# The second unit's v issued from ScalarE's queue instead of the sync engine, in attention followed by two MLPs

## The chip, the cores and the metric

One core of a Trainium2 chip. The metric is the device time of one execution of the whole kernel in microseconds (us), as the median of several runs.

## The reference

Inputs are q, k and v of 8 batches, 8 heads, 576 positions and 64 features, in 32-bit floats, and the weights of two MLPs (512 to 2048 to 512). What is computed, cut to what matters:

```python
q_s = softmax(q, axis=-1)            # over the 64 features, sum + 1e-9
k_s = softmax(k, axis=2)             # over the 576 positions, sum + 1e-9
kv  = einsum('bhsd,bhse->bhde', k_s, v)
x   = einsum('bhsd,bhde->bhse', q_s, kv)   # laid out as 4608 x 512
h = x @ w_in;  g = h * clip(h + 3, 0, 6) / 6;  x = g @ w_out     # first MLP
h = x @ w2_in; g = h * sigmoid(h);             out = g @ w2_out  # second MLP, 4608 x 512
```

## The kernel before, in words

The matmuls of the MLPs run at the rate of a one-pass format. To keep 32-bit accuracy each operand is split into an upper part and the rest, and each product is made of three matmuls. The 4608 tokens are nine blocks of 512. The stages are: `first_block` (the attention for block 0, the conversion of the first MLP's weights and the first MLP of block 0, with attention units of block 1 in between), `middle` (the rest of the first MLP and the attention, in an order written out in the table `MIDDLE`), and `second_mlp` (fixed passes, most of the time). Only the order of the first stage is planned, at build time.

**A unit** u of attention is a pair of heads of one token block. Units 0 to 3 give block 0. Its steps, each one method with its line: loads of k (L355, L359), v (two DMAs at L366 and a tail at L370) and q (L381); on VectorE the maxima (`q_max` L488, `k_max` L419 to L421); on TensorE `k_turn` L426 and, behind VectorE's `k_peak` L432, `k_spread` L438; the subtractions (`q_sub` L496 on GpSimd, `k_sub` L447 on VectorE); the exponentials on ScalarE (`q_exp` L506, `k_exp` L457); the sums and the normalisation of q (`q_norm` L522 on GpSimd); `q_turn` L530 and `q_copy` L555; the product k·v (`kv_mm` L466 on TensorE, `kv_sum` L474 and L475 on VectorE, `kv_scale` L483 on ScalarE); `x_mm` L567 on TensorE, its upper part copied by ScalarE (`x_upper` L581) and the rest made either on VectorE (L586) or by one more matmul and a copy (`x_rest` L594, `x_lower_copy` L601 on ScalarE). Matmuls at L933 on a tile `busy` are filler without a result, early in the stage.

**A weight** comes by a DMA on the sync engine (SP; L161 for w_in into `wi_early`, L155 for w_out into `wo_early`) and is split by `Conv`: two ScalarE steps (L176, L180), three VectorE steps (L188, L195, L199), ScalarE's `upper` (L216), then the rest (L220) on VectorE or GpSimd.

**One f** of the first MLP (f = 0 to 15, 128 of the 2048 hidden features): `mm1`, 12 matmuls at L613 into one of **two** PSUM banks `h`; the gate, which is `relu` L626 (ScalarE, into the **only** buffer `r`), `times_h` L653 (VectorE, reads `r`), `upper` L644 (ScalarE), `rest` L659 (one matmul), `lower_copy` L664 (ScalarE, gives the bank back); then `mm2`, 12 matmuls at L688.

**What sets the order.** `unit`, the weight conversions and the f steps add jobs to a `Plan`: an engine, an estimated duration in us, a key (how early it is wanted), the jobs it depends on, and the buffer tags that it takes and gives back. `plan.run` then works through them like a clock with one job at a time on every engine. Whatever each engine can start gets started in the order of the keys. The jobs are emitted in the planned order, and on the chip each engine runs its instructions in that order and waits at the first that isn't ready. A load counts as a job of 1.9 us of the queue it is put on (`"SP"` or `"AQ"`, ScalarE's queue). The instructions themselves, their number and their operands, do not depend on the plan.

Of the kernel before, what the change touches and what calls it, by code (L numbers as in the profile page):

```python
# [82 lines left out]
def efficient_attention_then_two_mlps(  # L83
# [267 lines left out]
    def load_k(u, eng=nc.sync):  # L351
        b, pr = divmod(u, NP)
        t = kbuf[u] = kbuf.get(u, kbuf[u % 2])
        src = k[b, 2 * pr : 2 * pr + 2]
        eng.dma_start(  # L355
            t[:, :, 0:KCH, :],
            src[:, 0 : KCH * P].rearrange("h (p j) d -> p h j d", j=KCH),
        )
        eng.dma_start(t[0:TAIL, :, KCH, :], src[:, KCH * P :].rearrange("h p d -> p h d"))  # L359

    def load_v(u, eng=nc.sync):
        b, pr = divmod(u, NP)
        t = vbuf[u] = vbuf.get(u, vbuf[u % 2])
        src = v[b, 2 * pr : 2 * pr + 2]
        for h in range(2):
            eng.dma_start(  # L366
                t[:, 0:KCH, h, 0:D],
                src[h, 0 : KCH * P].rearrange("(p j) d -> p j d", j=KCH),
            )
        eng.dma_start(  # L370
            t[0:TAIL, KCH, :, 0:D],
            src[:, KCH * P :].rearrange("h p d -> p h d"),
        )

    def load_q(u, eng=nc.sync):
        j, pr = divmod(u, NP)
        t = early.pop(("q", u), None)
        if t is None:
            t = att.tile([P, 2, NCH, D], F32, tag="q", bufs=2, name="qraw")
        for p0, n, b, s0 in parts(j):  # L380
            eng.dma_start(  # L381
                t[p0 : p0 + n],
                q[b, 2 * pr : 2 * pr + 2, s0 : s0 + NCH * n, :].rearrange(
                    "h (p i) d -> p h i d", i=NCH
                ),
            )
        qt[u] = t
# [97 lines left out]
    def q_max(u):  # L485
        t = qt[u]
        m = tiny.tile([P, 2, NCH, 1], F32, tag="qm", bufs=2, name="qm")
        nc.vector.tensor_reduce(out=m[:, :, :, 0], in_=t, op=ALU.max, axis=AX.X)  # L488
        live["qm", u] = m
# [14 lines left out]
    def q_exp(u):  # L504
        e = live["qe", u]
        nc.scalar.activation(e, e, AF.Exp)  # L506

    def q_sum(u):
        e = live["qe", u].rearrange("p i h d -> p (i h) d")
        s = tiny.tile([P, 2 * NCH, 1], F32, tag="qs", bufs=2, name="qs")  # L510
        nc.vector.tensor_reduce(out=s[:, :, 0], in_=e, op=ALU.add, axis=AX.X)
        live["qs", u] = s
# [280 lines left out]
    class Plan:  # L793
# [7 lines left out]
        def add(self, eng, us, key, fn, deps=(), take=(), give=(), port=False):  # L801
            self.jobs.append(
                (eng, us, key, fn, [d for d in deps if d is not None], list(take), list(give), port)
            )
            return len(self.jobs) - 1
# [104 lines left out]
    def first_block():  # L910
# [5 lines left out]
        def load(u, key, what, eng="SP", deps=()):  # L916
            e = nc.sync if eng == "SP" else nc.scalar
            if what == "q" and u == 0:
                n_q[u] = add(eng, 0.5, key, (lambda: None, 262144), deps)
            elif what == "k":  # L920
                n_k[u] = add(eng, 1.0, key, (lambda: load_k(u, e), 327680), deps)
            elif what == "q":
                n_q[u] = add(eng, 0.5 if u < NP else 1.1, key, (lambda: load_q(u, e), 262144), deps)
            else:
                n_v[u] = add(eng, 1.9, key, (lambda: load_v(u, e), 327680), deps)
# [12 lines left out]
        def turning(name, u, fn):  # L938
            return lambda: (fn(), spin((name, u)))

        def unit(u, key, until=7):
            small = u < NP
            bank = "h" if small else "a"
            pool = h_psum if small else a_pool
            qe = "g" if small else "qe"
            ke = "ke2" if small and u % 2 else "ke"
            qm = add("DVE", 0.68, key(0), lambda: q_max(u), [n_q[u]])
            km = add("DVE", 1.0, key(0), lambda: k_max(u), [n_k[u]], ["m1", "t2k"], ["t2k"], True)
            if until <= 1:
                return  # L950
            kt = add("PE", 0.2, key(1), turning("k_turn", u, lambda: k_turn(u, pool)), [km], [bank], ["m1"])
            kd = add("DVE", 0.3, key(1), lambda: k_peak(u), [kt], ["mx"], [bank])
            qs = add("POOL", 1.1, key(1), lambda: q_sub(u, nc.gpsimd), [qm], [qe], [], True)
            qsub[u] = qs
            if until <= 2:
                return
            ks = add("PE", 0.25, key(2), turning("k_spread", u, lambda: k_spread(u, pool)), [kd], [bank], ["mx"])
            kb = add("DVE", 0.82, key(2), lambda: k_sub(u), [ks], [ke], [bank])
            ksub[u] = kb
            qx = add("ACT", 0.65, key(2), lambda: q_exp(u), [qs])  # L960
            qa = add("DVE", 0.68, key(2), lambda: q_sum(u), [qx])
            qa = add("POOL", 0.25, key(2), lambda: q_eps(u, nc.gpsimd), [qa])
            qa = add("DVE", 0.2, key(2), lambda: q_recip(u), [qa])
            qn = add("POOL", 1.1, key(2), lambda: q_norm(u, nc.gpsimd), [qa], [], [], True)
            if until <= 3:
                return
            kx = add("ACT", 0.75, key(3), lambda: k_exp(u), [kb])
            qt_ = add("PE", 0.65, key(3), turning("q_turn", u, lambda: q_turn(u)), [qn], ["a"], [qe])
            ql = add("ACT", 0.6, key(3), lambda: q_copy(u), [qt_], ["qT"], ["a"])
            pkb = f"y{u}" if small else "a"  # L970
            mm = add(
                "PE", 1.0, key(4), turning("kv", u, lambda: kv_mm(u, y_psum(u) if small else a_pool)),
                [kx, n_v[u]], [pkb], [ke],
            )
            kvmm[u] = mm
            va = add("DVE", 0.35, key(4), lambda: kv_sum(u), [mm])
            vl = add("ACT", 0.65, key(4), lambda: kv_scale(u), [va], [], [pkb])
            xm = add("PE", 1.0, key(5), turning("x", u, lambda: x_mm(u)), [ql, vl], ["a"], ["qT"])
            xu = add("ACT", 0.6, key(5), lambda: x_upper(u), [xm])
            if u in DIRECT_X:  # L980
                xlow[u] = add("DVE", 0.69, key(5), lambda: x_lower(u), [xu], [], ["a"])
                return
            xr = add("PE", 0.23, key(5), turning("x_rest", u, lambda: x_rest(u)), [xu])
            xlow[u] = add("ACT", 0.6, key(5), lambda: x_lower_copy(u), [xr], [], ["a"])
# [3 lines left out]
        s0 = -30.0  # L988
# [2 lines left out]
        load(0, s0 + 0.2, "v", "AQ")  # L991
        load(1, s0 + 0.3, "k")
        load(1, s0 + 0.4, "q")
        load(1, s0 + 0.5, "v")
        for u in range(2, NP):
            for i, what in enumerate("kqv"):
                load(u, s0 + u + 0.1 * i, what)
# [43 lines left out]
        u = NP + 4  # L1041
# [835 lines left out]
```

## Time and profile before

| | us |
|---|---|
| median of 3 runs (lowest to highest) | 1552.95 (1552.77 to 1553.42) |
| the profiled execution | 1553.21 |
| its span, first to last instruction | 1551.5 |
| TensorE busy in the span | 1537.7 |
| VectorE, ScalarE, GpSimd busy | 1193.8, 781.3, 569.3 |

The profiled execution has 1.7 us around its span and lies 0.26 us above the median. Busy time is the sum over an engine's instructions. Waits are found in the timeline of an engine, where each row has its start, its time, and in brackets the idle time before it with the instruction that ended it. The granted clock is the share of TensorE's full clock in a stretch: 1.00 is 2.4 GHz and 0.50 is 1.2 GHz.

### The profile page before, as it was taken

To read this page: it belongs to the slowest core of one execution; us is meant where nothing else is said; L and a number is where in the kernel's file an instruction comes from. 1 tells how busy PE (TensorE), PEld (TensorE's weight loads), DVE (VectorE), ACT (ScalarE), POOL (GpSimd) and SP (SyncE) were. 2 spreads that over 40 slices of the span, in tenths; PEclk is the share of its full clock that TensorE was granted. 3 is DMA by queue.
4 is the path that set the end of the run, shared out by engine and by line. 5 is a ranking of instruction groups with operands and counts; after the bars stand their busy time and mean duration, and the time that the engine had idled before them with its cause. 6 is when DMAs were issued, how large, how long until landed. Compare 5 with 4: busy or idle time off the path is not lost.

```text
span 1551.5 us, 22340 instructions
## 1 busy us (share of the span) xinstructions
PE 1537.7 (99%) x7307; PEld 1254.3 (81%) x7307; DVE 1193.8 (77%) x1864; ACT 781.3 (50%) x1406; POOL 569.3 (37%) x490
## 2 busy tenths in 40 slices
PE   8999999999999999999999999999999999999999
PEld 5787888787788788888888888888888888888887
DVE  7988777888778878986798789867976797677632
ACT  6886344545455545654564456434643464345422
POOL 4333443565455725224623462234224422330000
PEclk9999999999999999999999999999999999999999
DMA  9914678788899788777877887687768766879850
GB/s 268 354 45 145 209 241 261 225 277 273 271 300 323 255 299 301 241 251 271 288 244 241 286 269 256 195 220 225 242 198 224 230 230 198 227 231 363 261 129 27
DMA packets 361459, 372.17 MB, mean 240 GB/s; under 512 B 127360, under 2 KB 253056, under 8 KB 361344
## 3 DMA queue, kind: packets, MB, share of 16 engines
q1 hardware_dynamic: 359728, 370.07, 74.7%
q8 instruction: 58, 0.95, 0.3%
q10 hardware_dynamic: 1616, 0.69, 0.2%
q14 instruction: 57, 0.47, 0.1%
HBM read 276.56 MB, written 94.11 MB: 239 GB/s over the span
## 4 chain that ended last, share of the span: by engine, by line
PE 93%; DVE 2%; ACT 1%; DMA 1%; POOL 1%; issue 0%; SPq 0%; DVEq 0%; POOLq 0%; ACTq 0%
PE pb L1428 29%; PE pb L1587 29%; PE h L613 15%; PE y L688 12%; PE y L690 3%; PE pa L567 2%; PE pa L466 1%; DMA wi_early<-in_moe_w_in_dram 1%; DVE basis L420 0%; DMA ws<-sp 0%; PE pa L530 0%; POOL qe L496 0%; DMA qraw<-in_q_dram 0%; PE busy L933 0%; POOL wi L220 0%
## 5 line engine op out<-in xcount | busy, mean ns | idle before, releaser
L1428 PE MATMUL pb<-xo,ring 128*128 128x512 f32 x2016 | 459.1, 389 | 0.0
L1587 PE MATMUL pb<-gsp,ring 128*128 128x512 f32 x2016 | 458.9, 389 | 0.0
L1428 PEld LDWEIGHTS pb<-xo,ring 128*128 128x128 f32 x2016 | 378.3, 188 | 78.7
L1587 PEld LDWEIGHTS pb<-gsp,ring 128*128 128x128 f32 x2016 | 378.4, 188 | 78.6
L613 PE MATMUL h<-x,wi 128*128 128x512 f32 x1152 | 292.1, 398 | 2.0 <-POOL wi L220 0.9
L613 PEld LDWEIGHTS h<-x,wi 128*128 128x128 f32 x1152 | 211.5, 188 | 50.6 <-POOL wi L220 1.9
L1415 DVE TENSOR_TENSOR gsp<-g,gsp 128x512 fp32r<-128x512 f32 x288 | 221.5, 787 | 26.7 <-ACT gsp L1533 25.9
L688 PE MATMUL y<-g,wo 128*128 128x512 f32 x960 | 236.8, 394 | 0.0
L1533 ACT CAST gsp<-g 128x512 fp32r<-128x512 f32 x288 | 171.9, 621 | 122.1 <-PE pb L1587 106.4
L688 PEld LDWEIGHTS y<-g,wo 128*128 128x128 f32 x960 | 178.0, 188 | 38.6 <-DVE g L647 0.2
L1415 POOL TENSOR_TENSOR xst<-xst 128x512 f32<-128x512 f32 x40 | 89.9, 2249 | 207.2 <-DVE xo L1415 112.1
L1415 POOL TENSOR_TENSOR s<-U,s 128x512 f32<-128x512 f32 x40 | 53.2, 1330 | 195.9 <-DVE U L1415 195.9
L1415 POOL TENSOR_TENSOR g<-g 128x512 f32<-128x512 f32 x48 | 64.3, 1339 | 133.2 <-DVE g L1415 64.5
L1442 ACT ACTIVATE r<-pb 128x512 f32<-128x512 f32 x96 | 56.9, 593 | 91.1 <-DVE pb L1415 69.6
L1415 DVE TENSOR_TENSOR g<-r,pb 128x512 f32<-128x512 f32 x96 | 65.5, 683 | 41.9 <-ACT r L1442 41.1
L626 ACT ACTIVATE r<-h 128x512 f32<-128x512 f32 x80 | 47.8, 597 | 72.9 <-PE h L613 66.3
L1415 DVE TENSOR_TENSOR U<-pb,s 128x512 f32<-128x512 f32 x96 | 65.8, 686 | 15.4 <-PE pb L1428 13.4
L644 ACT CAST g<-h 128x512 fp32r<-128x512 f32 x80 | 46.8, 585 | 54.7 <-DVE h L653 43.1
L1415 POOL TENSOR_TENSOR spare<-g,g 128x512 f32<-128x512 f32 x48 | 69.2, 1442 | 3.8
L653 DVE SCALAR_TENSOR_TENSOR h<-r,h 128x512 f32<-128x512 f32 x80 | 55.0, 687 | 19.0 <-ACT r L626 18.8
L1442 ACT ACTIVATE r<-s 128x512 f32<-128x512 f32 x32 | 20.2, 633 | 85.7 <-POOL s L1415 85.7
L496 POOL TENSOR_TENSOR qe<-qraw,qm 128x512 f32<-128x512 f32 x34 | 38.4, 1131 | 62.0 <-DVE qz L538 32.1
(198 smaller groups left out, 1905.8 us busy)
## 6 DMA issues: line engine op xcount, KB each, us to landing
ring<-ws SPq DMA_DIRECT2D x336, 512.0 KB, 4.1
ws<-sp SPq DMA_DIRECT2D x92, 256.0 KB, 3.1
wi_early<-in_moe_w_in_dram SPq DMA_DIRECT2D x16, 512.0 KB, 8.5
wo_early<-in_moe_w_out_dram SPq DMA_DIRECT2D x16, 512.0 KB, 9.5
wi_raw<-in_moe_w_in_dram SPq DMA_DIRECT2D x16, 512.0 KB, 4.7
ws<-w_sum SPq DMA_DIRECT2D x32, 256.0 KB, 3.0
xst<-yd SPq DMA_DIRECT2D x32, 256.0 KB, 4.8
wi<-ws SPq DMA_DIRECT2D x32, 256.0 KB, 5.8
```

The source lines that it names most:

```text
L496: eng.tensor_tensor(out=e.rearrange("p i h d -> p h i d"), in0=qt.pop(u), in1=live.pop(("qm", u)).to_broadcast([P, 2, NCH, D]), op=ALU.sub ...
L613: nc.tensor.matmul(h, w[:, a, c, :], x[:, e, c, :], start=(c == 0 and n == 0), stop=(c == NC - 1 and n == 2),)
L626: nc.scalar.activation(self.r, self.h, AF.Relu, bias=3.0)
L644: nc.scalar.copy(self.g[:, 0], self.r)
L653: nc.vector.scalar_tensor_tensor(out=self.h, in0=self.r, scalar=6.0, in1=self.h, op0=ALU.min, op1=ALU.mult)
L688: nc.tensor.matmul(y[c], w[:, a, cs], g[:, e, :], start=st, stop=sp)
L690: nc.tensor.matmul(y[c], g[:, e, cs], w[:, a, :], start=st, stop=sp, skip_group_check=c == NC - 1,)
L1415: (eng or nc.vector).tensor_tensor(out=out, in0=a, in1=b, op=how)
L1428: nc.tensor.matmul(to, ws_[:, a], e[:, c], start=p in ("P1", "P6", "P5") and c == 0 and m == 0, stop=c == 1 and m == 2, skip_group_check=True,
L1442: nc.scalar.activation(r, d[b, n, key], AF.Sigmoid)
L1533: nc.scalar.copy(t[0], source(p, i))
L1587: nc.tensor.matmul(d[b, p][m], w[:, a, m * P : (m + 1) * P], t[e], start=new and i == 0 and k == 0, stop=i == NPR - 1 and k == 2, skip_gro ...
```

## The change

The load of unit 1's v leaves the list of loads at the start, where it was put on SP behind unit 1's q, and is added inside `unit(0)`, on ScalarE's queue, with `q_exp` of unit 0 as its dependence.

```diff
             qx = add("ACT", 0.65, key(2), lambda: q_exp(u), [qs])
+            if u == 0:
+                load(1, s0 + 0.5, "v", "AQ", [qx])
             qa = add("DVE", 0.68, key(2), lambda: q_sum(u), [qx])
...
         load(1, s0 + 0.3, "k")
         load(1, s0 + 0.4, "q")
-        load(1, s0 + 0.5, "v")
         for u in range(2, NP):
```

Lines of the changed kernel are 2 higher between the two places and 1 higher behind the second; the methods named above keep their lines. The planner works with the new jobs, so the order on all engines changes up to the end of the first stage. The instructions are the same in kind and number; the table `MIDDLE` and the second MLP stay.

**Place one, the start.** On ScalarE (the difference between the two, - before and + now; `qe` and `ke` are the tiles of the exponentials of q and k):

```order
 L366 DMA vbuf<-in_v_dram 128x4x64 x2
 L370 DMA vbuf<-in_v_dram 64x2x64
 L506 ACTIVATE qe<-qe 128x512
+L366 DMA vbuf<-in_v_dram 128x4x64 x2
+L370 DMA vbuf<-in_v_dram 64x2x64
 L457 ACTIVATE ke<-ke 128x640 x2
 L483 ACTIVATE kvs<-pk,small 64x64 x2
```

Three DMAs now stand between ScalarE's first exponential of q and its first of k. On SP, in the same place of the program (`ahead` are the buffers for units 2 and 3):

```order
 L359 DMA kbuf_96<-in_k_dram 64x2x64
 L381 DMA qraw<-in_q_dram 128x2x256
-L366 DMA vbuf<-in_v_dram 128x4x64 x2
-L370 DMA vbuf<-in_v_dram 64x2x64
 L355 DMA ahead<-in_k_dram 128x2x256
 L359 DMA ahead<-in_k_dram 64x2x64
```

SP goes from unit 1's q straight to unit 2's k. The eight counters `DMAHW0` to `DMAHW7` are taken in turn by the DMAs of both queues, and a DMA waits for the landing of the one that last had its counter. In the changed kernel, ScalarE's three moved DMAs and then SP from unit 3's k on:

```order
L366 DMA vbuf<-in_v_dram 128x4x64 [waits DMAHW2_49]
L366 DMA vbuf<-in_v_dram 128x4x64 [waits DMAHW4_49]
L370 DMA vbuf<-in_v_dram 64x2x64 [waits DMAHW6_49]
...
L355 DMA ahead<-in_k_dram 128x2x256 [waits DMAHW2_49]
L359 DMA ahead<-in_k_dram 64x2x64 [waits DMAHW3_49]
L381 DMA ahead<-in_q_dram 128x2x256 [waits DMAHW4_49]
L366 DMA ahead<-in_v_dram 128x4x64 [waits DMAHW5_49,DVE_49]
L366 DMA ahead<-in_v_dram 128x4x64 [waits DMAHW6_49]
```

The moved DMAs hold counters 2, 4 and 6, and on SP unit 3's k, its q and its second v wait for the same three.

**Place two, where block 0's x is finished and the first MLP begins.** On TensorE before:

```order
L530 MATMUL pa<-basis,qe 128x128 x4
L567 MATMUL pa<-qt,kvs 128x512
L466 MATMUL pk<-ahead,ke 64x65 x10
L613 MATMUL h<-x,wi 128x512 x6
L530 MATMUL pa<-basis,qe 128x128 x4
L613 MATMUL h<-x,wi 128x512 x3
L567 MATMUL pa<-qt,kvs 128x512
L594 MATMUL pa<-x,minus 128x512
L613 MATMUL h<-x,wi 128x512 x15
```

And now:

```order
L466 MATMUL pk<-ahead,ke 64x65 x10
L933 MATMUL busy<-minus 128x512
L530 MATMUL pa<-basis,qe 128x128 x4
L466 MATMUL pk<-ahead,ke 64x65 x10
L530 MATMUL pa<-basis,qe 128x128 x4
L567 MATMUL pa<-qt,kvs 128x512 x2
L594 MATMUL pa<-x,minus 128x512
L613 MATMUL h<-x,wi 128x512 x24
```

All 24 `mm1` matmuls of f = 0 and 1 now stand behind the `x_mm` of units 2 and 3 and the `x_rest` of unit 3, where 9 of them stood ahead of unit 3's `x_mm` before.

**Place three, the gate of f = 4.** On ScalarE before, from f = 4's `relu` to its `lower_copy`:

```order
L626 ACTIVATE r<-h 128x512
L216 CAST wi<-fa 128x512
L176 ACTIVATE fa<-wo_early 128x512
L180 ACTIVATE fr<-wo_early 128x512
L644 CAST g<-h 128x512
L626 ACTIVATE r<-h 128x512
L664 CAST g<-h 128x512
```

And now:

```order
L626 ACTIVATE r<-h 128x512
L216 CAST wi<-fa 128x512
L176 ACTIVATE fa<-wo_early 128x512
L180 ACTIVATE fr<-wo_early 128x512
L626 ACTIVATE r<-h 128x512
L176 ACTIVATE fa<-wo_early 128x512
L180 ACTIVATE fr<-wo_early 128x512
L644 CAST g<-h 128x512
L216 CAST wo<-fa 128x512
L664 CAST g<-h 128x512
```

The `relu` of f = 5 and one more begin of a weight stand ahead of f = 4's `upper`, and a weight's `upper` stands ahead of its `lower_copy`. On VectorE in the same place, before:

```order
L199 SCALAR_TENSOR_TENSOR fa<-wi_early,fa 128x512
L220 TENSOR_TENSOR wi<-fa,wi 128x512
L188 TENSOR_SCALAR fa<-fa 128x512
L653 SCALAR_TENSOR_TENSOR h<-r,h 128x512
L447 TENSOR_TENSOR ke<-kbuf_95,pa 128x2x5x64
L195 ISA fa<-fa,fr 128x1024
```

And now:

```order
L199 SCALAR_TENSOR_TENSOR fa<-wi_early,fa 128x512
L188 TENSOR_SCALAR fa<-fa 128x512
L220 TENSOR_TENSOR wi<-fa,wi 128x512
L195 ISA fa<-fa,fr 128x1024
L653 SCALAR_TENSOR_TENSOR h<-r,h 128x512
L447 TENSOR_TENSOR ke<-kbuf_95,pa 128x2x5x64
L653 SCALAR_TENSOR_TENSOR h<-r,h 128x512
L199 SCALAR_TENSOR_TENSOR fa<-wo_early,fa 128x512
```

`times_h` of f = 4 (the first L653) now comes behind the rounding step L195 of a weight, and that of f = 5 before any other work on that weight. The order around f = 7 changes in the same way: nine steps stand between its `relu` and its `upper` on ScalarE (three before), and its `lower_copy` L664 stands behind an L216, which needs a sign step L199 that stands on VectorE behind `times_h` L653 and `k_sub` L447.

## Rows read from the trace of the kernel before

**Rows 1.** The page, part 1: busy time, share of the span, instructions.

```profile
PE 1537.7 (99%) x7307; PEld 1254.3 (81%) x7307; DVE 1193.8 (77%) x1864; ACT 781.3 (50%) x1406; POOL 569.3 (37%) x490
```

**Rows 2.** Windows: length, busy PE, PEld, DVE, ACT, POOL; PEclk, DMA share, GB/s.

```profile
5.00:10.00 5.00, 3.14 (x11) 1.68 (x9) 4.64 (x11) 0.63 (x1) 1.32 (x2) 0.92 1.04 262
10.00:15.00 5.00, 4.87 (x44) 3.55 (x44) 3.54 (x11) 3.21 (x6) 3.08 (x3) 0.50 0.81 206
15.00:20.00 5.00, 4.79 (x25) 2.89 (x23) 3.61 (x11) 2.53 (x7) 1.64 (x3) 0.90 0.95 282
...
26.00:35.00 9.00, 6.51 (x40) 3.31 (x39) 8.51 (x16) 8.65 (x18) 3.81 (x4) 1.00 1.02 290
35.00:58.00 23.00, 22.73 (x100) 18.27 (x100) 22.14 (x38) 19.99 (x38) 7.33 (x7) 1.00 1.03 379
58.00:64.00 6.00, 5.66 (x42) 3.98 (x40) 5.80 (x8) 5.58 (x11) 3.25 (x3) 1.00 1.05 406
...
84.00:92.00 8.00, 8.00 (x55) 6.45 (x54) 7.63 (x16) 6.93 (x14) 3.08 (x3) 1.00 0.04 10
...
130.00:142.00 12.00, 11.62 (x66) 9.22 (x66) 8.57 (x20) 7.54 (x15) 2.33 (x4) 1.00 0.56 178
```

**Rows 3.** Timeline of SP, 0 to 20 us: start, time of issuing, queue, line, out<-in, count.

```profile
4.54 1.25 SPq L366 DMA_DIRECT2D vbuf<-in_v_dram  x2
6.45 0.62 SPq L370 DMA_DIRECT2D vbuf<-in_v_dram  x1
...
11.09 0.59 SPq L355 DMA_DIRECT2D ahead<-in_k_dram  x1
...
15.04 0.59 SPq L161 DMA_DIRECT2D wi_early<-in_moe_w_in_dram  x1
```

**Rows 4.** DMAs issued from 4.5 to 4.6 us: median us from issue to landing.

```profile
vbuf<-in_v_dram SPq DMA_DIRECT2D x1, 128.0 KB, 4.3
```

**Rows 5.** Timeline of ScalarE, 6 to 20 us: start, time, line, out<-in, [idle before <-releaser].

```profile
6.78 0.63 ACT L506 ACTIVATE qe<-qe 128x512 f32<-128x512 f32 x1 [3.98 <-POOL qe L496]
10.10 0.74 ACT L457 ACTIVATE ke<-ke 128x640 f32<-128x640 f32 x1 [2.69 <-DVE ke L447]
...
19.92 0.68 ACT L176 ACTIVATE fa<-wi_early 128x512 f32<-128x512 f32 x1 [0.46 <-DMA wi_early<-in_moe_w_in_dram]
```

**Rows 6.** Timeline of TensorE, 14 to 39 us.

```profile
14.18 1.35 PE L466 MATMUL pk<-vbuf,ke 128*64 128x65 f32 x20
...
26.40 0.80 PE L466 MATMUL pk<-ahead,ke 128*64 128x65 f32 x20
...
34.80 3.50 PE L613 MATMUL h<-x,wi 128*128 128x512 f32 x14 [0.45 <-ACT x L601]
38.14 0.39 PE L659 MATMUL h<-g,minus 128*128 128x512 f32 x1
```

**Rows 7.** Timeline of GpSimd, the rest of f = 1's first weight.

```profile
34.16 1.52 POOL L220 TENSOR_TENSOR wi<-fa,wi 128x512 fp32r<-128x512 f32 x1 [3.73 <-ACT wi L216]
```

**Rows 8.** Timeline of ScalarE at the gate of f = 4, first and last of seven steps.

```profile
56.29 0.60 ACT L626 ACTIVATE r<-h 128x512 f32<-128x512 f32 x1 [0.39 <-PE h L613]
...
59.71 0.59 ACT L664 CAST g<-h 128x512 fp32r<-128x512 f32 x1
```

**Rows 9.** Timeline of VectorE there.

```profile
55.37 0.69 DVE L195 CUSTOM_DVE_ANT_0 fa<-fa,fr 128x1024 uint16<-128x1024 uint16 x1
...
57.65 0.69 DVE L653 SCALAR_TENSOR_TENSOR h<-r,h 128x512 f32<-128x512 f32 x1
58.24 0.81 DVE L447 TENSOR_TENSOR ke<-kbuf,pa 128x640 f32<-128x640 f32 x1
```

**Rows 10.** Timeline of TensorE there.

```profile
56.12 2.98 PE L613 MATMUL h<-x,wi 128*128 128x512 f32 x12
59.17 0.51 PE L659 MATMUL h<-g,minus 128*128 128x512 f32 x1
59.95 0.66 PE L530 MATMUL pa<-basis,qe 128*128 128x128 f32 x4 [0.28 <-POOL qe L522]
```

## The prediction

> **What bounds the kernel now.** The busy times come first: TensorE works for 1537.7 of 1551.5 us, and VectorE, next, for 77% [rows 1]. So a change can win at most what TensorE idles, and it loses whatever it makes TensorE idle. The windows of the first stage come second, because the diff touches that stage alone. Read the PE column against the length. From 26 to 35 us TensorE has 6.51 of 9 us, from 35 to 58 it has 22.73 of 23, from 58 to 64 it has 5.66 of 6, from 84 to 92 all of it, and from 130 to 142 it has 11.62 of 12 [rows 2]. VectorE and ScalarE are close behind in the same windows: 22.14 and 19.99 of 23 [rows 2]. That matters most here. In this stage three engines are nearly full at once and each runs its list strictly in order, so an order that puts one step of a gate late has no slack to hide it. The clock column comes third: 0.92, 0.50 and 0.90 from 5 to 20 us, 1.00 in the other windows shown [rows 2]. The timelines around the places that the change moves come last.
>
> **The moved DMAs.** SP loses three issues, 1.25 us for two and 0.62 us for the third, 1.87 us [rows 3]. ScalarE gets them behind its `q_exp` at 6.78 + 0.63 = 7.41 us, and behind them waits `k_exp`, which in the trace stood idle for 2.69 us and began at 10.10 when VectorE's `ke` was ready [rows 5]. Three issues of at most 1.87 us end by 9.3, so they lie inside that wait and cost ScalarE nothing (without that cover they would cost their 1.87 us). v itself was issued at 4.54 and needs 4.3 us from issue to landing [rows 3, 4]. Issued between 7.4 and 9.3 it lands by 13.6 at the latest, and its user, the second `kv_mm`, runs at 14.18 [rows 6]. So the load costs nothing. What does SP gain? Its issues behind v move up, but unit 3's k, q and second v share counters with the three moved DMAs and wait for their landing. The first of those lands at 7.4 + 4.3 = 11.7 at the latest, and SP issued that k at 11.09 before [rows 3]. So from that k on, SP wins between 0 and 1.87 us, and the first weight, issued at 15.04 [rows 3], comes 0.3 to 0.8 us sooner. I take 0.6. ScalarE's first begin of a weight waited 0.46 us for that DMA and ran at 19.92 [rows 5]; it moves to about 19.3.
>
> **The moved order** is the larger part. The planner counts 1.9 us less on SP and none of the shared counters, and it deals the work of all engines out anew. I went through both orders in program order, with the durations of the trace, and four places differ for TensorE.
>
> *Block 0's x.* From the first weight's begin to `q_copy` of unit 3, ScalarE now has 19 instructions. At 18 in 8.65 us, 0.48 each [rows 2], these end at 19.3 + 9.1 = 28.4, or up to 29.0 with a wait. `x_mm` of unit 3, two conversions, its upper copy and `x_rest` bring the first `mm1` to about 30.9. All 24 `mm1` matmuls are now behind that. Before, 9 of them filled the time. Since the last `kv_mm`, which ran at 26.40 for 0.80 us [rows 6], TensorE has only three short pieces of matmul, about 0.5 us of 4. At the other end f = 1 needs its weight. That is nine ScalarE steps, 4.3 to 5.1 us behind `q_copy`, then GpSimd's rest of 1.52 us [rows 7], so about 35 us, where before it was 34.16 + 1.52 = 35.7. The 24 matmuls then end about 0.4 us earlier than the 38.14 [rows 6] of before: **−0.4 us** (bounds −1.0 and +0.5), with the idle time in one piece instead of several.
>
> *The gate of f = 4.* Before, `relu` at 56.29 and `rest` at 59.17 are 2.88 us apart, and `mm1` of f = 5, from 56.12 for 2.98 us, covers all of it [rows 8, 10]. Now the one buffer `r` ties the two gates together. `relu` of f = 5 waits for `times_h` of f = 4, that for the rounding step in front of it, that for the weight's begin. The chain is `relu`, L216, L176, L180 on ScalarE, L195 and L653 on VectorE, then L626, L176, L180 and L644 on ScalarE. ScalarE made six steps from 56.29 to 59.71, 0.57 each [rows 8]; VectorE's two take 0.69 each [rows 9]. Eight by 0.57 and two by 0.69 are 5.9 us, and 0.3 more for the sign step that L216 waits for: 6.2. On TensorE there is 2.8 us of `mm1` and 0.4 of a transposition that in any case waited [rows 10]. It idles 3.0. Behind it `mm1` of f = 6 needs a bank, which L664 gives back two steps (1.1 us) after `upper`, with 0.2 of `rest` beside them: 0.9 more. Less the 0.34 that this window idles now [rows 2], **+3.5 us** (bounds +2.5 and +4.5).
>
> *The gate of f = 7.* `lower_copy` waits for L653, `k_sub` (0.81) and L199 on VectorE, then L216 and itself on ScalarE: 0.69 + 0.81 + 0.69 (L199 taken at the price of L195) + 2 x 0.57 = 3.3 us [rows 8, 9], with about 0.6 of TensorE work beside. Before, this window idles nothing [rows 2]: **+2.6 us** (bounds +1.5 and +3.3).
>
> *The attention pieces around 137 us* stand one behind the other without `mm1` between. The window has 0.38 us of idle time now [rows 2]. I put **+0.6 us** (bounds 0 and +1.5), and **−0.3 us** (down to −0.6) for the 0.27 us of waits from 35 to 58 us [rows 2] that come into other orders.
>
> The sum of the stalls is −0.4 + 3.5 + 2.6 + 0.6 − 0.3 = **+6.0 us**. All low bounds together give +2.4, all high ones +9.5; I use +4 to +8. Nothing later absorbs it, since `MIDDLE` and the second MLP run the same instructions with TensorE full.
>
> **The clock.** Between 5 and 10 us TensorE was busy for 3.14 of 5 us, and from there the clock fell: 0.92, 0.50, 0.90 over three windows [rows 2]. The same product of k and v took 1.35 us at 14.18 and 0.80 at 26.40 [rows 6]. The bill of that stretch is 5 x (0.08 + 0.50 + 0.10) = 3.4 us of full-clock time. The new holes, some 0.5 us of work in 4 and 0.6 in 5, are emptier than that one. I take one such stretch after each of the first two holes. After the second, it costs the full 3.4 us. After the first, the 24 matmuls, 24 x 0.24 = 5.7 us at 14 in 3.34 [rows 6], run in a stretch of 6.8 us that waits for weights anyway, so 1.1 of it is hidden: 2.3. Together **+5.6 us** (bounds 0 and +9.1, with a third stretch after f = 7). The Trainium skill ("TensorE: Matmul & The Clock Gate", Part 1) has it that the throttled state is the default and activity releases it. By that rule all three holes would be paid for, +9.1 us, and the sum would be that of the third rival. The trace agrees only in part: at 26 to 35 us TensorE idles 2.5 of 9 us at 1.00 [rows 2].
>
> **Sum.** 1553.21 + 6.0 + 5.6 = 1564.8 for a profiled execution; that one stood 0.26 above its median, so **1564.5 us**.
>
> **Rivals.**
>
> *Stalls without the clock.* The holes stay at 1.00 as 26 to 35 us did. 1552.95 + 6.0 = 1559.0, with the stalls' bounds 1557 to 1561.
>
> *A third half-clock stretch* behind f = 7: 1564.5 + 3.5 = 1568. For it speaks that this hole is in itself just as empty; against it, that it is short.
>
> *No change.* The gates lose less than I sum, or the weights, sooner by up to 1.87 us, give it back at the next f: 1553, within 3 us. Against it speak 22.14 and 19.99 of 23 us on VectorE and ScalarE [rows 2], which leave about 1 us of slack in 23 on VectorE.
>
> *Faster.* The weight stream is what TensorE waits for in this stage. It comes 1.87 us sooner, and the idle time of the windows shown closes: 2.5 us at 26 to 35, then 0.27, 0.34 and 0.38 [rows 2], together 3.5 us. 1552.95 − 3.5 = 1549.5. It decides if the weights gain all of SP's 1.87 us and the two gates lose nothing against `mm1` of the f behind them. For it speaks that ScalarE did wait 0.46 us for the first weight [rows 5]; against it, that SP waits for the landing of the very DMAs that were moved. The Trainium skill ("DMA: Bandwidth & Descriptors", "Issuing engines are not separate DMA queues") says that a second issuing engine saves only the time that the first spends on issuing. By that rule alone the move would be worth at most those 1.87 us, 1551.1, and belong to no change; no row here contradicts it.
>
> **How the numbers follow.** Stalls and clock as summed 0.50; stalls alone 0.24; third stretch 0.08; no change 0.12; faster 0.06. The range from 1556 to 1569 leaves out the last two and little else. 0.2% is 3.1 us, about what a measurement of this kernel can tell from no change. Faster by more than that comes only with the last case, 0.06; within it 0.12; slower 0.82.
>
> **What would show it.** At the start: three DMAs on ScalarE between 7.4 and 9.4 us, `k_exp` still near 10.1, the first weight's issue near 14.5. Between 27 and 31 us a TensorE hole of over 3 us, ended by ScalarE's copies. Near 59 to 63 us waits of together about 4 us in front of `rest` and the `mm1` behind it, near 85 to 88 some 2.6 us, and a clock near 0.5 behind the first two. From 200 us on nothing differs but the shift. I am wrong if the three holes together add less than 3 us of idle time, or if the shift of the two kernels' instructions grows behind 200 us.

## The result, and the profile after

| | us |
|---|---|
| changed kernel, median of 4 runs (lowest to highest) | 1567.38 (1566.44 to 1568.92) |
| before, median of 4 runs (lowest to highest) | 1553.18 (1552.77 to 1553.57) |
| ratio, with its 95% interval | 1.0092 (1.0079 to 1.0105) |
| span of the profiled execution, after and before | 1565.4 and 1551.5 |

The change costs 14 us, 0.9%. Where they are lost is read from windows cut at the same events in both traces: 26 us, then the starts of `mm2` of f = 0, 1, 2, 3, 7 and of the 17th `mm2` (the first behind the first block). In each row: length, busy time of TensorE, its weight loads, VectorE, ScalarE and GpSimd, the granted clock, and the DMA share. Before:

```profile
26.00:38.37 12.37, 9.88 (x55) 5.95 (x53) 11.75 (x20) 11.14 (x22) 7.18 (x6) 1.00 0.98 285
38.37:44.62 6.25, 5.98 (x27) 4.62 (x26) 6.05 (x10) 6.02 (x12) 2.17 (x3) 1.00 1.05 392
44.62:50.31 5.69, 5.69 (x27) 4.66 (x26) 5.38 (x12) 4.41 (x8) 0.00 (x0) 1.00 1.07 401
50.31:64.05 13.74, 13.40 (x78) 10.34 (x76) 13.32 (x21) 12.65 (x23) 5.09 (x4) 1.00 1.05 402
64.05:84.39 20.34, 20.23 (x91) 15.65 (x88) 18.29 (x34) 16.65 (x32) 4.64 (x4) 1.00 0.61 192
84.39:148.97 64.58, 64.20 (x379) 51.64 (x377) 53.79 (x104) 50.48 (x95) 22.72 (x23) 1.00 0.27 79
```

After:

```profile
26.00:40.01 14.01, 11.41 (x33) 7.43 (x32) 10.91 (x18) 10.67 (x21) 4.55 (x4) 0.76 1.01 310
40.01:50.64 10.63, 7.59 (x26) 5.71 (x25) 9.07 (x14) 7.82 (x14) 3.09 (x3) 0.84 1.06 401
50.64:56.34 5.70, 5.70 (x27) 4.67 (x26) 4.70 (x9) 2.87 (x5) 0.00 (x0) 1.00 1.05 397
56.34:71.93 15.59, 12.04 (x52) 9.07 (x50) 13.85 (x21) 13.10 (x24) 5.41 (x4) 0.96 1.03 371
71.93:96.10 24.17, 23.25 (x114) 18.16 (x113) 22.06 (x39) 18.85 (x36) 6.64 (x6) 0.95 0.16 38
96.10:163.05 66.95, 64.83 (x378) 51.68 (x377) 52.25 (x97) 48.24 (x91) 21.61 (x21) 1.00 0.26 77
```

Subtract row from row. The length grows by 1.6, 4.4, 0.0, 1.9, 3.8 and 2.4 us: 14.1 in all by the 17th `mm2`, against 13.9 in the span. Idle time is length less TensorE's busy time. It grows by 0.1, 2.8, 0, 3.2, 0.8 and 1.7 us, together 8.6. The length times what the clock lacks of 1.00 gives 3.4, 1.7, 0, 0.6, 1.2 and 0: 6.9 us. The two together are 15.5; the first window gives back 1.9 of that, because more of TensorE's work was done ahead of 26 us, and the last holds 0.6 us more work. Work also moved from the fourth window to the fifth: at full clock the fourth holds 2.0 us less of it than before and the fifth 1.8 more. So the fourth, with f = 4's gate, lost 3.8 us although it grew by 1.9, and the fifth 2.0 of the 3.8 that it grew by.

The lines that answer to [rows 6] and [rows 10], TensorE's timeline after, with the waits in brackets:

```profile
26.11 1.03 PE L567 MATMUL pa<-qt,kvs 128*128 128x512 f32 x2
29.03 1.41 PE L567 MATMUL pa<-qt,kvs 128*128 128x512 f32 x2 [1.89 <-ACT qt L555]
31.12 0.80 PE L594 MATMUL pa<-x,minus 128*128 128x512 f32 x1 [0.68 <-ACT x L581]
31.71 7.92 PE L613 MATMUL h<-x,wi 128*128 128x512 f32 x24
...
45.97 0.50 PE L659 MATMUL h<-g,minus 128*128 128x512 f32 x1 [3.04 <-ACT g L644]
...
66.73 0.66 PE L530 MATMUL pa<-basis,qe 128*128 128x128 f32 x4 [1.56 <-POOL qe L522]
68.70 0.50 PE L659 MATMUL h<-g,minus 128*128 128x512 f32 x1 [1.32 <-ACT g L644]
69.88 2.25 PE L613 MATMUL h<-x,wi 128*128 128x512 f32 x6 [0.68 <-ACT g L664]
...
94.14 0.49 PE L659 MATMUL h<-g,minus 128*128 128x512 f32 x1 [0.25 <-ACT g L644]
95.30 0.96 PE L613 MATMUL h<-x,wi 128*128 128x512 f32 x3 [0.68 <-ACT g L664]
```

The holes at 27 to 31 us (waits of 1.89 and 0.68 us) and at 65 to 70 us were forecast, and so was one at f = 7, which is smaller than forecast. The 3.04 us in front of `rest` of f = 1 were not. The clock fell three times:

```profile
29.00:37.00 8.00, 7.29 (x17) 4.98 (x18) 5.84 (x10) 5.08 (x10) 2.64 (x2) 0.57 0.98 279
46.00:51.00 5.00, 5.00 (x15) 4.00 (x16) 4.28 (x9) 4.02 (x8) 0.60 (x1) 0.66 1.05 410
70.00:75.00 5.00, 5.00 (x15) 3.94 (x16) 4.69 (x6) 3.21 (x6) 2.92 (x3) 0.66 0.34 81
```

8 x 0.43, 5 x 0.34 and 5 x 0.34 make 3.4, 1.7 and 1.7 us. Each of the three windows lies behind one of the holes.

How `relu` of f = 5 came to wait at f = 4's gate is read from ScalarE and VectorE after, to be set against [rows 8] and [rows 9]:

```profile
64.31 0.65 ACT L180 ACTIVATE fr<-wo_early 128x512 uint32<-128x512 uint32 x1
66.47 0.60 ACT L626 ACTIVATE r<-h 128x512 f32<-128x512 f32 x1 [1.51 <-DVE h L653]
63.98 1.79 DVE L195 CUSTOM_DVE_ANT_0 fa<-fa,fr 128x1024 uint16<-128x1024 uint16 x1
65.69 0.68 DVE L653 SCALAR_TENSOR_TENSOR h<-r,h 128x512 f32<-128x512 f32 x1
```

The rounding step L195 in front of `times_h` began ahead of ScalarE's L180 and took 1.79 us, where it takes 0.69 by itself [rows 9].

At the start, SP and ScalarE did what the change says. SP after, where unit 3's k and the first weight stood at 11.09 and 15.04 [rows 3]:

```profile
10.74 0.59 SPq L355 DMA_DIRECT2D ahead<-in_k_dram  x1
...
14.70 0.59 SPq L161 DMA_DIRECT2D wi_early<-in_moe_w_in_dram  x1
```

ScalarE after, against [rows 5]:

```profile
6.66 0.63 ACT L506 ACTIVATE qe<-qe 128x512 f32<-128x512 f32 x1 [3.85 <-POOL qe L496]
6.67 1.24 ACTq L366 DMA_DIRECT2D vbuf<-in_v_dram  x2
8.44 0.64 ACTq L370 DMA_DIRECT2D vbuf<-in_v_dram  x1
9.98 0.74 ACT L457 ACTIVATE ke<-ke 128x640 f32<-128x640 f32 x1 [2.69 <-DVE ke L447]
```

The three issues begin beside `q_exp` and end at 9.08 us, ahead of `k_exp`, whose wait for `ke` is 2.69 us in both. Of SP's 1.87 us of issuing, 0.34 us came back at the first weight in this execution. That is inside the spread: in the profiles of the other runs below that issue the load on ScalarE behind `q_exp` the first weight was issued between 13.88 and 15.10 us.

### The profile page after: what moved, and what is told of

The parts are those of the page before. It is cut to its first block, busy times and chain, and to the rows that moved or that the text cites. A ratio compares the mean times of both kernels' runs of the same rounds, so it can differ in the third digit from the quotient of the medians.

```text
span 1565.4 us, 22337 instructions
## 1 busy us (share of the span) xinstructions
PE 1543.3 (99%) x7307; PEld 1259.3 (80%) x7307; DVE 1197.9 (77%) x1864; ACT 782.3 (50%) x1406; POOL 569.5 (36%) x490
## 4 chain that ended last, share of the span: by engine, by line
PE 95%; DVE 2%; ACT 1%; DMA 1%; issue 0%; POOL 0%; SPq 0%; DVEq 0%; POOLq 0%; ACTq 0%
PE pb L1429 29%; PE pb L1588 29%; PE h L613 16%; PE y L688 13%; PE y L690 3%; PE pa L567 2%; PE pa L466 1%; DVE fa L195 0%; DVE fa L188 0%; PE busy L933 0%; PE h L659 0%; DVE fa L199 0%; DMA qraw<-in_q_dram 0%; PE pa L426 0%; DMA vbuf<-in_v_dram 0%
## 5 line engine op out<-in xcount | busy, mean ns | idle before, releaser
L613 PE MATMUL h<-x,wi 128*128 128x512 f32 x1152 | 295.5, 402 | 2.0 <-ACT g L664 2.0
L613 PEld LDWEIGHTS h<-x,wi 128*128 128x128 f32 x1152 | 215.3, 191 | 50.6 <-ACT g L664 3.0
L653 DVE SCALAR_TENSOR_TENSOR h<-r,h 128x512 f32<-128x512 f32 x80 | 55.0, 688 | 25.2 <-ACT r L626 24.9
```

The costliest lines, as they stand in the source:

```text
L613: nc.tensor.matmul(h, w[:, a, c, :], x[:, e, c, :], start=(c == 0 and n == 0), stop=(c == NC - 1 and n == 2),)
L653: nc.vector.scalar_tensor_tensor(out=self.h, in0=self.r, scalar=6.0, in1=self.h, op0=ALU.min, op1=ALU.mult)
```

## The experiments

The first two runs ask whether the moved DMAs cost the time or the order that the planner deals out behind them.

Two spreads limit what the later runs can say. The changed kernel's four times lie 2.5 us apart, so a difference of 1 or 2 us between medians of four is not clear of the spread. And in the profiled executions of the runs with the change's order, ScalarE began the first weight at 18.93 to 20.42 us, a time that no edit explains. A start of `mm2` therefore compares between two profiles only to about 1.5 us, unless it is counted from that begin: 18.93 us in the change.

**The move alone.** The planner counts the load as before, so every other instruction keeps its place:

```diff
-                n_v[u] = add(eng, 1.9, key, (lambda: load_v(u, e), 327680), deps)
+                n_v[u] = add(eng, 1.9, key, (lambda: u == 1 or load_v(u, e), 327680), deps)
...
-            qx = add("ACT", 0.65, key(2), lambda: q_exp(u), [qs])
+            qx = add("ACT", 0.65, key(2), lambda: (q_exp(u), u == 0 and load_v(1, nc.scalar)), [qs])
```

> v of unit 1 is issued from ScalarE behind the first q exponential, but the plan still counts the load on SP, so that every engine's other instructions stand in the order of before. Theory 'the order costs': within 0.1% of before, about 1553 us; the first weight is issued near 14.7 us and TensorE's windows are those of before, clock 1.00 from 26 us on. Rival 'the moved DMAs cost' (shared counters, ScalarE's queue): near the change, 1560 us or more. Rival 'SP's time is worth something': 1551 us or less.

Measured: 1552.45 us (11 runs, 1551.82 to 1553.49) against 1553.08 for before, ratio 0.9997 (0.9988 to 1.0006). The first weight was issued at 14.53 us, 0.5 us sooner than before, and every `mm2` up to f = 7 started within 0.1 us of before's. So the DMAs in ScalarE's queue, behind `q_exp`, cost nothing and win nothing that can be measured.

**The order alone.** The plan of the change, with the load issued on SP as before:

```diff
-                n_v[u] = add(eng, 1.9, key, (lambda: load_v(u, e), 327680), deps)
+                n_v[u] = add(eng, 1.9, key, (lambda: u == 1 or load_v(u, e), 327680), deps)
...
-(lambda: load_q(u, e), 262144), deps)
+(lambda: (load_q(u, e), u == 1 and load_v(1, nc.sync)), 262144), deps)
```

> The plan of the change, order and all, but v of unit 1 is issued on SP where before issued it, behind unit 1's q. Theory 'the order costs': 12 to 16 us over before, 1565 to 1569 us, with half-clock stretches behind TensorE holes near 29, 45 and 68 us. Rival 'the moved DMAs cost': near before, 1553 to 1556 us.

Measured: 1568.22 us, ratio 1.0098 (1.0084 to 1.0111), with waits of 1.87, 3.05, 1.54, 1.33 and 0.68 us at the change's places and the clock at half near 32, 46 and 70 us. The order carries the whole loss.

**Filler in the first hole.** Eight filler matmuls behind the x product of unit 2 and six behind that of unit 3, into a PSUM bank that is free there:

```diff
-("kv", 2): 1, ("x", 1): 1,
+("kv", 2): 1, ("x", 1): 1, ("x", 2): 8, ("x", 3): 6,
```

> The change with 14 filler matmuls on TensorE in the hole at 27 to 31 us (8 behind the x product of unit 2, 6 behind that of unit 3), without a result. Theory 'the hole at 43 to 46 us is a consequence of the half clock behind the first hole': the clock stays 1.00 up to 60 us, the first 24 mm1 take about 5.7 us, the wait of 3.04 us in front of the rest of f = 1 shrinks below 0.6 us, and the time is 5 to 6.5 us less than the change, about 1561.5 us. Rival 'the order itself makes the hole at 43 us': only the 1.6 us that the first mm2 was late come back, the wait stays near 3 us and is followed by half clock, about 1565.5 us.

Measured: 1566.00 us, ratio to before 1.0083 (1.0069 to 1.0097). The rival was right. The clock stayed at 1.00 up to the next hole, but TensorE then waited for weights instead, and the hole at f = 1 stayed, with 2.13 us. TensorE's waits in this run:

```profile
35.65 0.73 PE L613 MATMUL h<-x,wi 128*128 128x512 f32 x2 [0.58 <-ACT wi L216]
37.01 2.56 PE L613 MATMUL h<-x,wi 128*128 128x512 f32 x10 [0.63 <-POOL wi L220]
...
44.65 0.50 PE L659 MATMUL h<-g,minus 128*128 128x512 f32 x1 [2.13 <-ACT g L644]
```

`mm2` of f = 1 started at 49.31 instead of 50.64 us, 1.3 us sooner, or 2.0 counted from the first weight, which began at 19.59 here. That is what came back for a first half-clock stretch of 3.4 us by its windows.

**f = 4's gate as before.** In the planned list of jobs, f = 4's `times_h` goes behind its `relu`, its `upper` ahead of f = 5's `relu`, `rest` and `lower_copy` behind that. On ScalarE this gives the rows of place three as they stood before; on VectorE `times_h` comes ahead of L188 and L220, two steps earlier than it stood before:

```diff
             jobs = self.jobs
+            if hasattr(self, "gate"):
+                (r0, t0, u0, x0, l0), r1 = self.gate
+                order.remove(t0), order.insert(order.index(r0) + 1, t0)
+                order.remove(u0), order.insert(order.index(r1), u0)
+                order.remove(x0), order.insert(order.index(r1) + 1, x0)
+                order.remove(l0), order.insert(order.index(x0) + 1, l0)
```

> The change with one place of its order put back as before: around f = 4's gate, times_h directly behind its predecessors, upper ahead of f = 5's relu, rest and lower_copy next, the rest of the order as in the change. Theory 'this gate's order costs about 3.3 us up to the fifth mm2, and its half-clock stretch 1.7 of them': 3 to 5 us less than the change, about 1563.5 us, with the clock 1.00 from 52 us on. Rival 'the engines are behind anyway and the wait moves to the next gate': within 1.5 us of the change.

Measured: 1565.71 us, ratio 1.0081 (1.0065 to 1.0096), 1.7 us under the change, which is nearer the rival and not clear of the spread. Its profile tells more. TensorE's timeline:

```profile
31.44 1.12 PE L567 MATMUL pa<-qt,kvs 128*128 128x512 f32 x2 [1.86 <-ACT qt L555]
33.24 0.50 PE L594 MATMUL pa<-x,minus 128*128 128x512 f32 x1 [0.68 <-ACT x L581]
...
45.66 0.50 PE L659 MATMUL h<-g,minus 128*128 128x512 f32 x1 [2.24 <-ACT g L644]
...
65.16 0.50 PE L659 MATMUL h<-g,minus 128*128 128x512 f32 x1 [1.90 <-ACT g L644]
...
93.34 0.96 PE L613 MATMUL h<-x,wi 128*128 128x512 f32 x3 [1.24 <-ACT g L664]
```

And two of its windows cut as above:

```profile
26.00:40.53 14.53, 10.62 (x59) 6.85 (x59) 13.59 (x26) 14.00 (x28) 6.70 (x5) 1.00 1.00 305
...
67.97:94.13 26.16, 23.29 (x114) 17.44 (x114) 25.34 (x41) 21.02 (x39) 7.95 (x7) 1.00 0.29 87
```

The holes near 30 and 44 us are there, and the clock stayed at 1.00 behind all of them. So such a hole does not always bring half clock, and an execution without it was still slow. The waits at f = 4 shrank and came back later: from the third to the eighth `mm2` it took 39.7 us, as in the change (39.8; before 34.1). That is the rival's account.

**The step of f = 1.** With the filler, `times_h` of f = 1 moved directly behind its `relu` in the list, which on VectorE puts it one step (L188) earlier:

```diff
+                r1, t1 = self.gate
+                order.remove(t1), order.insert(order.index(r1) + 1, t1)
```

> The change with the 14 filler matmuls of the run before and one VectorE step moved: times_h of f = 1 stands one weight step (L188) earlier, as near to its relu as the program allows. Theory 'the hole at f = 1 is the order of VectorE, whose steps GpSimd stretches': that L188 took 1.5 us beside a GpSimd step, so the wait in front of the rest of f = 1 falls from 2.13 to about 0.7 us, the half-clock stretch behind it goes (1.7 us), and mm2 of f = 1 starts 3 us sooner than in the run with the filler alone; at the end 2 to 3 us are left of it, about 1563.5 us. Rival 'weights are late anyway': mm2 of f = 1 starts sooner, but the next gates wait so much longer and the time stays within 1 us of the filler's run, about 1565.5 us.

Measured: 1563.20 us, ratio 1.0067 (1.0052 to 1.0082), 2.8 us under the filler's run (single executions of the two overlap, 1562.58 to 1565.28 against 1564.30 to 1566.74). The first theory fits. `mm2` of f = 1 started at 45.71 us, 3.6 sooner, with 0.87 us of wait and no half clock behind it, and 3.6 of it are still there at the 17th `mm2`. Of the 3.6, 0.75 was there at `mm2` of f = 0, ahead of the moved step, and is not its work: the step itself is worth 2.85. Why one step is worth so much is read from VectorE's timeline in the changed kernel:

```profile
37.55 0.70 DVE L653 SCALAR_TENSOR_TENSOR h<-r,h 128x512 f32<-128x512 f32 x1 [2.32 <-ACT r L626]
38.15 1.79 DVE L195 CUSTOM_DVE_ANT_0 fa<-fa,fr 128x1024 uint16<-128x1024 uint16 x1
39.98 1.42 DVE L199 SCALAR_TENSOR_TENSOR fa<-wi_early,fa 128x512 uint32<-128x512 uint32 x1
41.32 0.41 DVE L188 TENSOR_SCALAR fa<-fa 128x512 uint32<-128x512 uint32 x1
41.87 0.69 DVE L195 CUSTOM_DVE_ANT_0 fa<-fa,fr 128x1024 uint16<-128x1024 uint16 x1
42.59 0.69 DVE L199 SCALAR_TENSOR_TENSOR fa<-wi_early,fa 128x512 uint32<-128x512 uint32 x1
43.20 1.49 DVE L188 TENSOR_SCALAR fa<-fa 128x512 uint32<-128x512 uint32 x1
44.62 0.68 DVE L653 SCALAR_TENSOR_TENSOR h<-r,h 128x512 f32<-128x512 f32 x1
```

And GpSimd's there:

```profile
38.10 1.29 POOL L220 TENSOR_TENSOR wo<-fa,wo 128x512 fp32r<-128x512 f32 x1 [2.12 <-ACT wo L216]
39.36 1.49 POOL L496 TENSOR_TENSOR qe<-qraw,qm 128x512 f32<-128x512 f32 x1
42.76 1.65 POOL L220 TENSOR_TENSOR wi<-fa,wi 128x512 fp32r<-128x512 f32 x1 [1.91 <-ACT wi L216]
```

VectorE waits 2.32 us for the late first `relu`, and then three of the six weight steps take 1.4 to 1.8 us beside GpSimd. By themselves such steps take 0.4 to 0.7, as the three rows between show. `times_h` of f = 1 stands behind all six. The late `relu` is the smaller part: in the filler's run VectorE did not wait for it, and 2.13 of the 3.04 us were left.

**Place two in part.** Six of the first `mm1` matmuls ahead of unit 3's x product, and the first weight's `upper` and rest directly behind its sign step:

```diff
+                (sign, upper, lower), mm, xm = self.first
+                order.remove(upper), order.insert(order.index(sign) + 1, upper)
+                order.remove(lower), order.insert(order.index(upper) + 1, lower)
+                for m in mm:
+                    order.remove(m), order.insert(order.index(xm), m)
```

> The change with place two put back in part: six of the first mm1 matmuls stand ahead of the x product of unit 3 again, and the first weight's upper and rest stand directly behind its sign step. The gates of f = 1, 4 and 7 stand as in the change. Theory 'each gate's order has its own price': mm2 of f = 0 starts 1 to 2 us sooner than in the change, but the holes at f = 1 and f = 4 stay, and the time is 1 to 3 us less, 1564 to 1566 us. Rival 'the late start of the first mm1 sets off everything behind': ScalarE's and VectorE's waits of 2.3 us in front of the first gate go, the later holes with them, and the time falls by 6 us or more, to 1561 us or less.

Measured: 1565.38 us, ratio 1.0078 (1.0061 to 1.0095). The time is that of the first theory, the way there was neither's. `mm2` of f = 0 started at 41.70, 1.7 us later than in the change, but the first weight had begun 1.5 later (20.42 us); counted from there it is 0.2. VectorE did not wait for the first `relu`, the idle time at f = 1 went to nothing, and `mm2` of f = 1 started at 47.63, 3.0 us sooner than in the change, with f = 1's `times_h` in the change's place. The idle time at f = 4 stayed as it was (3.5 us), with a half-clock stretch of 3.4 us behind it. So an earlier first `mm1` takes the loss at f = 1 away and leaves that at f = 4: the rival is right for the one and wrong for the other.

**f = 4 and f = 7 on top.** Both carry the filler and the step of f = 1. The first adds f = 4's gate as above, the second also the two moves below. Only the first of them, `times_h`, changed anything. `lower_copy` was put behind `rest`, but `rest` stands in the planned list behind the weight's `upper`, so ScalarE's order is that of the run before it:

```diff
+                (r0, t0, u0, x0, l0) = gate[7]
+                behind(t0, r0), behind(l0, x0)
```

> The run with the filler and the step of f = 1 moved, and f = 4's gate put back to the order of before as well. There the waits in front of f = 4's transposition, rest and next mm1 were 1.55, 1.32 and 0.68 us. Theory 'each gate's order has its own price': of 3.5 us of idle time and 1.7 us of half clock between the third and the sixth mm2 at least 2.5 us go and stay gone, about 1560 us. Rival 'behind f = 4 the weights are late, so the wait moves': the sixth to eighth mm2 are as late as without this edit and the time stays within 1 us of 1563.2.

> As the run before it, and at f = 7 times_h directly behind its relu and lower_copy directly behind its rest, ahead of the weight's upper. Theory 'own price': the 0.9 us of idle time at f = 7's gate go, 0.5 to 1 us less than the run before it. Rival 'the wait moves': the same time as the run before it.

Measured: 1563.77 (ratio 1.0066, 1.0051 to 1.0081) and 1564.41 us (1.0069, 1.0052 to 1.0086), against 1563.20 (1.0067) without either. For f = 4 the rival was right: the fourth `mm2` came 1.2 us sooner with f = 4's gate put back, the seventh 0.3, and the eighth 0.3 us later. For f = 7 the question was not put, since `lower_copy` did not move. ScalarE at f = 7 in that run:

```profile
89.78 0.62 ACT L216 CAST wo<-fa 128x512 fp32r<-128x512 f32 x1 [0.76 <-DVE fa L199]
90.31 0.58 ACT L664 CAST g<-h 128x512 fp32r<-128x512 f32 x1
```

The idle time at this gate was 1.8 us, against 1.5 in the run before it and 0.9 in the change. In the run with f = 4's gate VectorE is nearly full behind it, which fits a wait that moves; two windows of it:

```profile
51.75:66.37 14.62, 12.48 (x51) 9.63 (x50) 13.71 (x21) 12.12 (x23) 5.14 (x4) 0.91 1.06 403
66.37:91.47 25.10, 23.18 (x115) 17.70 (x114) 24.31 (x40) 19.95 (x37) 6.92 (x7) 0.99 0.37 113
```

VectorE is busy for 24.31 of 25.10 us. In before's window from f = 3 to f = 7 it was busy for 18.29 of 20.34. No run took work off VectorE, so that it is the limit there is argued and not shown.

**A buffer of its own for f = 4's `relu`.** The order of the change:

```diff
-            self.r = tmp.tile([P, BLK], F32, tag="r", bufs=1, name="r")
+            if self.s == (0, 0, 4):
+                self.r = att.tile([P, BLK], F32, tag="sp", bufs=3, name="r")
+            else:
+                self.r = tmp.tile([P, BLK], F32, tag="r", bufs=1, name="r")
```

> The change, in the change's order, but f = 4's relu writes a buffer of its own, so that f = 5's relu needn't wait for f = 4's times_h. Theory 'the one buffer r ties the two gates': f = 5's relu starts at about 65.2 instead of 66.5 us and f = 4's upper about 1.1 us sooner, rest with it; 1 us off the idle time there, so about 1566.5 us. Rival 'VectorE's late times_h is the tie': f = 5's relu moves but f = 4's upper and rest stay where they are, and the time is that of the change, 1567.4 us.

Measured: 1567.36 us, ratio 1.0088 (1.0073 to 1.0103), the change's time. The buffer did tie the gates: `rest` of f = 4 waited 0.17 instead of 1.32 us. But `lower_copy` still stands behind a weight's `upper`, which here waited 0.83 us for VectorE, and the wait for the bank behind it was 1.42 instead of 0.68. The waits at this gate came to 3.12 us instead of 3.56. Neither theory had that.

This run tells something else as well. Up to f = 4 its order is the change's, and its first weight began at 18.95 us, as in the change (18.93). But no half clock followed the first hole, whose waits were 1.87 and 0.67 us. `mm2` of f = 0 started at 38.82 instead of 40.01 us, and that of f = 1 at 48.45 instead of 50.64. Between these two executions the first half-clock stretch was worth 1.2 us at the first `mm2` and 2.2 at the second.

**The queue alone.** The planner too is told of ScalarE's queue, without the dependence:

```diff
-        load(1, s0 + 0.5, "v")
+        load(1, s0 + 0.5, "v", "AQ")
```

> The load of the second unit's v is put on ScalarE's queue for the planner too, but without the dependence on q_exp. The planner then leaves the order of TensorE, VectorE and GpSimd as before, and ScalarE issues the three DMAs ahead of its first q_exp. Theory 'the dependence redeals the order, and the order is what costs': within 0.2% of before, 1552 to 1555 us; ScalarE's first q_exp may start up to 1.5 us later, as the DMAs wait for landings in front of it, and that much of a shift at most is seen at the first mm2. Rival 'the queue costs': near the change, 1560 us or more.

Measured: 1554.43 us (11 runs), ratio 1.0009 (1.0000 to 1.0018), 1.3 us over before, with an interval that begins at nothing. TensorE, VectorE and GpSimd have before's order row for row. ScalarE's first `q_exp` starts at 8.56 instead of 6.78 us, behind DMAs that wait for landings, and in the profiled execution, the slowest of the 11, `mm2` is 2.1 us late from f = 0 to f = 7. The other way round, given the dependence and SP's queue, the planner deals these three engines the change's order row for row; that kernel was not run. So it is the dependence on `q_exp`, not the queue, that redeals the order.

## Why the prediction was right, point by point

*The moved DMAs cost nothing*: shown, by the move alone (1552.45 us). Of the 0.6 us by which the first weight was to come sooner, 0.34 came in the change's execution and 0.5 in that of the move alone, which is inside the spread.

*The order costs*: shown, by the order alone. *Why* the planner redeals was put wrongly. "The planner counts 1.9 us less on SP" is not it: with only the queue changed, the plan counts the same 1.9 us less on SP and the order stayed. The dependence is.

*Block 0's x, −0.4 us, and 2.3 us of half clock*: together 1.9, measured 1.6 at the first `mm2`. The parts came out otherwise. The half-clock stretch was 3.4 us; where it did not come, in the run with the buffer, the first `mm2` started 1.2 us sooner, and still 0.45 later than before's and not 0.4 sooner, since TensorE then waited 0.62 and 0.63 us for the weights of f = 1. At the second `mm2` the stretch was worth 2.2, near the 2.3 forecast.

*The gate of f = 1* is the step that is missing. The prediction named four places, and this one, 4.4 us, is not among them; its −0.3 us for the waits from 35 to 58 us covers this stretch, which idled 2.8 us more and had 1.7 us of half clock. The prediction took VectorE's steps at their usual durations. Three of the steps in front of `times_h` took 1.4 to 1.8 us beside GpSimd, together 2.9 us more than usual, and the hole is 3.04. Two edits shrank or removed it: the moved step, and the earlier first `mm1`. From 20 to 170 us, sixteen weight steps on VectorE took over 0.3 us more than usual in the changed kernel, 13.2 us in sum, and ten in before, 8.1 us; each of them overlaps a GpSimd instruction. The Trainium skill ("SBUF — State Buffer", "Terms", shared port pair) says that these two engines share one pair of ports, which one instruction holds to its end. The rows agree. But the sum does not follow the time: it is 14.3 us in eighteen steps in the run with the step of f = 1 moved (1563.20 us), and 16.3 in twenty with f = 4's gate put back as well (1563.77 us). What a stretched step costs depends on what stands behind it, and no run here took GpSimd's work away, so the share of the collisions in the 14 us is open.

The planner does try to keep these two engines apart. Among its tags is `port`, of which there is one, and VectorE's weight steps and GpSimd's larger jobs each take it, so in the planned times they never run together. On the chip they do, in both orders.

*The gate of f = 4, +3.5 us*: the waits in front of the transposition, `rest` and the next `mm1` are 1.56, 1.32 and 0.68, 3.56 us. The figure is right and the tie through the one buffer `r` is there (`relu` of f = 5 waited 1.51 us for `times_h`), but the chain in front of it was another, so the exact hit is luck. The prediction has the rounding step wait for ScalarE's L216, L176 and L180; it began at 63.98 us, ahead of L180, and was late because it took 1.79 us in place of 0.69. The half-clock stretch there was 1.7 and not 3.4. That the order of this gate alone makes the loss did not hold: put back, the waits came again further on.

*The gate of f = 7, +2.6 us*: 0.93 us by its two waits, so sized too high. The prediction adds VectorE's three steps to the wait, but the last of them, the sign step, ended at 93.27 us, ahead of `upper` at 93.50; only ScalarE's L216 and `lower_copy` stood in the way. *The attention pieces near 137 us, +0.6*: three waits of 0.38, 0.39 and 0.68 us near 147 to 149 us, against one of 0.38 before, 1.1 more and inside the bounds. A wait of 0.68 us at 116.66 us was not forecast.

*The clock, +5.6 us*: three stretches instead of two, 6.8 us by their windows. They are not fixed by the order. In the profile of the order alone they lack 1.7, 1.7 and 1.7 us; in that of the buffer none follows the first hole, then 1.7 and 3.4, and 1.7 near 148 us; in that of the run with f = 4's gate as before none comes behind 26 us. The net price of all of them was not measured: the spans of the change, the order alone and the buffer are 1565.4, 1565.1 and 1565.7 us with 6.8, 5.1 and 6.8 us lacking.

*The sum* was 11.6 us, measured 14: stalls 8.6 and half clock 6.9, less 1.3 of shifted work, instead of 6.0 and 5.6. That it came so near is in part luck: f = 1's gate was missing and f = 7's too large, and the clock stretches lie elsewhere in each execution. What was reasoned and held is that the order costs and the load does not, that TensorE idles behind the gates, and that half clock follows some of the holes.

*The signs*: the hole between 27 and 31 us was 2.6 us and not over 3. The waits at f = 4 came at 65 to 70 us and not 59 to 63, since the `mm2` of f = 2 was already 6 us late. The three holes add more than 3 us of idle time, 4.1 by the windows that hold them. Behind the 17th `mm2` nothing is added: from there to the end of the span it is 1402.4 us, before 1402.5.

*Rivals*: "no change" and "faster" fell with the time and with the idle time at the gates. "A third half-clock stretch" came, at f = 1 and not at f = 7, and its forecast of 1568 lies nearest.

## What to carry to other kernels

Where a build-time planner sets the order, cost an edit by what the planner deals out anew, and separate the two by keeping the old order with the new instruction in it: here the instruction was free and the order cost 14 us. A plan that keeps two engines apart in its own times need not keep them apart on the chip: look for steps that take longer than usual in front of a gate. Putting back single pieces did not bring the order back: one step at f = 1 was worth 2.8 us, while f = 4's gate only moved the wait. A DMA can be moved to another queue without a dependence in the plan, but behind the step that its queue must not hold up: behind `q_exp` it cost nothing, ahead of it 1.3 us by the medians (0 to 2.8 by the interval).

## What was not expected of the hardware

A hole of the same form in TensorE's work did not always bring the half clock: behind 1.86 and 0.68 us of waits near 29 to 33 us the clock stayed at 1.00 in the run with f = 4's gate as before, and behind 1.89 and 0.68 us at the same place of the program it fell to 0.57 over 8 us in the change's. The two differ in what came before: the execution with f = 4's gate as before had a wait of 2.18 us near 18 us and ran from 20 to 26 us at 0.72, where the change's ran at 1.00. That this decides is not shown: in the run with the buffer, which also ran at 1.00 from 20 to 26 us, the clock stayed up behind the same hole. The changed order's executions lie further apart (1566.44 to 1568.92) than before's (1552.77 to 1553.57).
